# Float64 weights become float32 with three VectorE operations per piece in place of five

## The chip, the cores and the metric

The kernel runs on one core of a Trainium2 chip. The metric is the device time of one launch in microseconds (us), of which the median of three runs is taken. In the views of the profile PE is TensorE, PEld its weight loads, DVE is VectorE, ACT is ScalarE, POOL is GpSimd, and SP is the queue engine that issues most DMAs here; a name with q at its end (SPq) is the engine's sequencer.

## The reference

Attention over 12,288 tokens of 128 channels with pooled keys and values (768 keys), and behind it two expert layers, each with 2,048 hidden units. The four weight matrices of the experts arrive as float64.

```python
kv_pool = kv.reshape(B, H // r, r, W // r, r, C).mean(axis=(2, 4))
k = v = kv_pool.reshape(B, -1, C) @ w_sr
a = softmax(q @ k.transpose(0, 2, 1) / sqrt(C))
x = a @ v
h = x @ moe_w_in
x = (h * clip(h + 3, 0, 6) / 6) @ moe_w_out
h = x @ moe2_w_in
g = where(h >= 1, h, where(h <= -1, 0, (h + 1) ** 2 / 4))
out = g @ moe2_w_out
```

## The kernel before

**Products.** Each operand of a product is split into a rounded part (hi) and the rest (lo), and three products (hi·hi, hi·lo, lo·hi) accumulate in PSUM. So each pair of hidden blocks costs 6 matmuls of 128x128 by 128x512 into the layer and 6 out of it.

**Slots.** Tokens go in 24 blocks of 512, hidden units in 8 pairs of 128 per block. The main loop (`slot`, L582) runs over slots T: slot T does pair T of the first layer, pair T-11 of the second (so the second layer starts at slot 11), and a piece of attention for a later block. The order in which each engine gets its instructions is written out by hand and kept: in a slot ACT applies relu (L498), DVE multiplies (`mul1`, L504), ACT rounds the result (L532), POOL subtracts to get the lo part (L533); for the attention piece DVE takes the row maximum (L375), ACT the exponential (L400) and a scaled copy (L414), DVE the rest of that copy (L421). The second layer has `clip2` (L511), `sq2` (L517) and `max2` (L521). Each L504 needs the relu of its slot, the relu needs the matmuls L457, and these need a free PSUM buffer (there are four, given back by L504 and L521).

**Weights.** A piece of weights is 128 x 512 float64, loaded as pairs of 32-bit words into a staging buffer. There are 16 such jobs, j0 to j15, and each runs through four stages. Stage 0 to 2 turn the bits of float64 into float32 in the staging buffer; stage 3 rounds to hi on ACT (L192) and subtracts to lo on POOL (L194). Jobs j0 to j6 are placed among the steps before slot 0 (`PROLOGUE`, where `j4.2` means stage 2 of job 4); jobs j7 to j15 start in slots 0, 1, 4, 6, 7, 8, 10, 12 and 14 (`CONV_AT`). `conv_step` (L201), near the end of each slot, moves every running job by one stage, the oldest first, and then starts the new one. So a job that starts in slot T has its stages 1, 2 and 3 in slots T+1, T+2 and T+3. Behind `conv_step` a slot has only loads and matmuls, so the next thing on DVE is the softmax scale (two tiny operations, L408 and L411) and L504 of slot T+1, and on ACT it is the relu of slot T+1.

**Stages before.** DVE: stage 0 shifts the lower word (L161, tile wr) and shifts and flips the upper one (L162, wa); stage 1 makes a mask (L172, mk); stage 2 masks (L179) and joins the sign (L181). ACT: stage 0 squares the upper word (L164, mk), stage 1 rounds wr (L169). POOL: stage 1 adds wa and wr (L174). The tiles wa, wr and mk have two buffers each. The staging tiles are called t, h, l, g or wst after the buffer that they borrow; j12 to j15 use wst, which has two buffers, so that the loads of j14 and j15 wait for stage 3 of j12 and j13.

Of the kernel before, what the change touches and what calls it, by code (L numbers as in the profile page):

```python
# [8 lines left out]
FP32 = mybir.dt.float32  # L9
F32R = mybir.dt.float32r  # L10
FP16 = mybir.dt.float16
U32 = mybir.dt.uint32
I32 = mybir.dt.int32
ACTF = mybir.ActivationFunctionType
ALU = mybir.AluOpType
AX = mybir.AxisListType

W_MIN = 3.4332275390625e-05
O2, LAG2 = 11, 2
# LOADS: order of the loads (k: keys and values, w: next weights, q: queries of a block).  # L20
# PROLOGUE: order of the steps before slot 0; the table of steps stands above the slots' loop.
# CONV_AT: slots that start a weight conversion. EARLY: slots of attention for blocks 1 and 2
# (four scores, two products with V each) and of the transpose of block 2's queries.
LOADS = "w k0 k1 w k4 k6 k2 k5 k3 w q0 k8 k7 k9 k10 k11 w w w w w q1 w w w w w w q2 w w"
KV_MODE = "DDVVPPPPPPPP"
PROLOGUE = """
# [19 lines left out]
def tile_attn_moe_moe2(  # L46
# [11 lines left out]
    """Products run as float32r: an operand is split exactly into a rounded part (hi) and the  # L58
    rest (lo), and hi*hi + hi*lo + lo*hi accumulate in PSUM. The attention weights and V are
    split the same way into float16 parts, scaled by powers of two into float16's range."""  # L60
    nc = tc.nc
# [52 lines left out]
    # Jobs that end before slot 0 may use any staging buffer, those that end before slot O2 the  # L114
    # ones of the second layer, and the rest their own.
# [4 lines left out]
    # A staging buffer may be taken again once the last reader of what it holds is issued.  # L120
# [33 lines left out]
    # The upper words, read as float32, keep the order of the magnitudes: those whose square  # L154
    # reaches W_MIN ** 2 belong to weights of 2 ** -126 and more; others become zero.
    def w_stage0(job):
        t = wst[job][0]
        a = wk_p.tile([128, WP], U32, tag="wa", name="wa")
        r = wk_p.tile([128, WP], U32, tag="wr", name="wr")
        mk = wk_p.tile([128, WP], FP32, tag="mk", name="mk")  # L160
        nc.vector.tensor_scalar(out=r, in0=t[:, :, 0], scalar1=28, scalar2=None, op0=ALU.logical_shift_right)  # L161
        nc.vector.tensor_scalar(out=a, in0=t[:, :, 1], scalar1=3, scalar2=0x40000000,  # L162
                                op0=ALU.logical_shift_left, op1=ALU.bitwise_xor)
        nc.scalar.activation(out=mk, in_=t[:, :, 1].bitcast(FP32), func=ACTF.Square)  # L164
        wcv[job] = (a, r, mk)

    def w_stage1(job):
        a, r, mk = wcv[job]
        nc.scalar.activation(  # L169
            out=r.bitcast(I32), in_=r.bitcast(I32), func=ACTF.Copy, scale=0.5, bias=0.25  # L170
        )
        nc.vector.tensor_scalar(out=mk.bitcast(I32), in0=mk, scalar1=W_MIN ** 2, scalar2=-1.0,  # L172
                                op0=ALU.is_ge, op1=ALU.mult)
        nc.gpsimd.tensor_tensor(out=a.bitcast(I32), in0=a.bitcast(I32), in1=r.bitcast(I32), op=ALU.add)  # L174

    def w_stage2(job):
        a, r, mk = wcv.pop(job)
        hi32 = wst[job][0][:, :, 1]
        nc.vector.scalar_tensor_tensor(out=a, in0=a, scalar=0x7FFFFFFF, in1=mk.bitcast(U32),  # L179
                                       op0=ALU.bitwise_and, op1=ALU.bitwise_and)  # L180
        nc.vector.scalar_tensor_tensor(out=hi32, in0=hi32, scalar=0x80000000, in1=a,  # L181
                                       op0=ALU.bitwise_and, op1=ALU.bitwise_or)
# [136 lines left out]
    # DRAM rows are read and written in runs of 32 channels, so that transposes of 32 x 32  # L319
    # blocks within a partition group make [tokens, channels] from [channels, tokens] and back.  # L320
# [202 lines left out]
    def hi_lo(m, s):  # L523
        g = g_t.pop((m, s))
        # After the first layer's last pair the second one takes its buffers too.
        n = 1 if m == 0 or (s >= NS - O2 and s % 2) else 2
        hi = hl_p.tile([128, 2, 512], F32R, tag=f"h{n}", name=f"h{n}")
        lo = hl_p.tile([128, 2, 512], F32R, tag=f"l{n}", name=f"l{n}")
        hl_t[m, s] = hi, lo
        for k in range(2):  # L530
            eng = nc.vector if s == NS - 1 else nc.gpsimd
            nc.scalar.copy(out=hi[:, k], in_=g[:, k])  # L532
            eng.tensor_tensor(out=lo[:, k], in0=g[:, k], in1=f32(hi[:, k]), op=ALU.subtract)  # L533

# [1 line left out]
    # Slot T: pair T of the first layer, pair T - O2 of the second, and a piece of attention.  # L536
# [172 lines left out]
```

## Time and profile before

| | us |
|---|---|
| median of three runs | 1375.62 |
| lowest, highest | 1374.92, 1380.48 |
| the profiled execution, first to last instruction (span) | 1373.8 |

| engine | busy us | share of the span |
|---|---|---|
| PE | 1317.9 | 96% |
| DVE | 1188.8 | 87% |
| POOL | 1084.1 | 79% |
| ACT | 1033.1 | 75% |

The span of the profiled execution is 1.8 us under the median. The shares of the whole span say little about the change, since the weights are converted in the first 200 us only: there the loop has other limits than later, and the rows below cut the span at the points where these change. A row of the timeline gives the start of an instruction, its length, engine, line, operation and shape; in brackets stands the idle time of the engine ahead of it and what ended it. An instruction's length includes the time in which it was held up after it had started.

### The profile page before, as it was taken

To read this page: it belongs to the slowest core of one execution; us is meant where nothing else is said; L and a number is where in the kernel's file an instruction comes from. 1 tells how busy PE (TensorE), PEld (TensorE's weight loads), DVE (VectorE), ACT (ScalarE), POOL (GpSimd) and SP (SyncE) were. 2 spreads that over 40 slices of the span, in tenths; PEclk is the share of its full clock that TensorE was granted. 3 is DMA by queue.
4 is the path that set the end of the run, shared out by engine and by line. 5 is a ranking of instruction groups with operands and counts; after the bars stand their busy time and mean duration, and the time that the engine had idled before them with its cause. 6 is when DMAs were issued, how large, how long until landed. Compare 5 with 4: busy or idle time off the path is not lost.

```text
span 1373.8 us, 18492 instructions
## 1 busy us (share of the span) xinstructions
PE 1317.9 (96%) x6244; PEld 1077.0 (78%) x6244; DVE 1188.8 (87%) x1847; ACT 1033.1 (75%) x1917; POOL 1084.1 (79%) x826
## 2 busy tenths in 40 slices
PE   7478889999999999999999999999999999999998
PEld 6356668888888888888888888888888888888876
DVE  4899998789989989889888888898899899898777
ACT  2566787887777777777877777777877778777776
POOL 2367898888878878878878878888788788788887
PEclk9789899999999999999999999999999999999999
DMA  9442212212212122122222213222122121211000
GB/s 323 103 96 45 62 31 43 46 34 44 43 32 50 31 42 49 34 43 39 43 43 39 43 31 51 32 42 50 27 47 42 32 50 24 43 37 30 8 8 16
DMA packets 260783, 66.28 MB, mean 48 GB/s; under 512 B 252368, under 2 KB 256592, under 8 KB 260688
## 3 DMA queue, kind: packets, MB, share of 16 engines
q1 hardware_dynamic: 259456, 62.94, 23.2%
q10 hardware_dynamic: 1232, 2.16, 0.4%
q8 instruction: 49, 0.80, 0.2%
q14 instruction: 46, 0.38, 0.1%
HBM read 21.04 MB, written 6.29 MB: 20 GB/s over the span
## 4 chain that ended last, share of the span: by engine, by line
PE 86%; DVE 9%; issue 2%; ACT 1%; POOL 1%; DMA 1%; SPq 0%; DVEq 0%; POOLq 0%; ACTq 0%
PE acc L473 36%; PE h L457 36%; PE s L364 6%; PE s L436 6%; DVE wa L179 1%; PE h L245 1%; DVE t L504 1%; DVE g L521 1%; DVE g L511 1%; DVE a L421 1%; DMA h<-in_moe_w_out_dram 1%; POOL l L533 1%; DVE wa L162 1%; DVE wr L161 1%; DVE nm L375 0%
## 5 line engine op out<-in xcount | busy, mean ns | idle before, releaser
L533 POOL TENSOR_TENSOR l<-g,h 128x512 fp32r<-128x512 f32 x382 | 508.3, 1351 | 213.3 <-ACT h L532 155.7
L533 POOL TENSOR_TENSOR l<-t,h 128x512 fp32r<-128x512 f32 x382 | 501.8, 1335 | 24.6 <-ACT h L532 20.7
L498 ACT ACTIVATE t<-h 128x512 f32<-128x512 f32 x384 | 226.7, 597 | 215.5 <-PE h L457 207.6
L504 DVE SCALAR_TENSOR_TENSOR t<-t,h 128x512 f32<-128x512 f32 x384 | 248.6, 681 | 121.1 <-ACT t L498 121.0
L521 DVE TENSOR_TENSOR g<-h,g 128x512 f32<-128x512 f32 x384 | 245.6, 680 | 13.2 <-ACT g L517 6.4
L532 ACT CAST h<-t 128x512 fp32r<-128x512 f32 x384 | 224.9, 619 | 31.0 <-DVE t L504 27.7
L511 DVE TENSOR_SCALAR g<-h 128x512 f32<-128x512 f32 x384 | 245.8, 680 | 0.7 <-POOL l L533 0.4
L517 ACT ACTIVATE g<-g 128x512 f32<-128x512 f32 x384 | 228.1, 628 | 1.6 <-DVE g L511 1.3
L532 ACT CAST h<-g 128x512 fp32r<-128x512 f32 x384 | 217.7, 617 | 4.2 <-DVE g L521 3.6
L457 PE MATMUL h<-xh,wi0h 128*128 128x512 f32 x384 | 153.8, 400 | 9.2 <-DVE t L504 4.7
L473 PE MATMUL acc<-h,wo0h 128*128 128x512 f32 x384 | 156.5, 408 | 2.2 <-DVE su L408 2.2
L473 PE MATMUL acc<-l,wo0h 128*128 128x512 f32 x384 | 153.6, 400 | 4.8 <-POOL l L533 4.7
L457 PE MATMUL h<-xl,wi0h 128*128 128x512 f32 x384 | 153.7, 400 | 3.3 <-DVE xl L442 3.3
L457 PE MATMUL h<-x2h,wi1h 128*128 128x512 f32 x384 | 152.8, 398 | 2.2 <-DVE g L521 2.2
L457 PE MATMUL h<-xh,wi0l 128*128 128x512 f32 x384 | 152.9, 398 | 0.0
L473 PE MATMUL acc<-h,wo0l 128*128 128x512 f32 x384 | 152.5, 397 | 0.0
L457 PE MATMUL h<-x2h,wi1l 128*128 128x512 f32 x384 | 152.5, 397 | 0.0
L473 PE MATMUL acc<-h,wo1h 128*128 128x512 f32 x384 | 151.9, 396 | 0.6 <-DVE o L489 0.4
L457 PE MATMUL h<-x2l,wi1h 128*128 128x512 f32 x384 | 152.1, 396 | 0.0
L473 PE MATMUL acc<-l,wo1h 128*128 128x512 f32 x384 | 151.4, 395 | 0.0
L473 PE MATMUL acc<-h,wo1l 128*128 128x512 f32 x384 | 151.4, 394 | 0.0
L421 DVE SCALAR_TENSOR_TENSOR a<-e,rc,a 128x768 f16<-128x768 f32 x96 | 137.7, 1434 | 2.8
(139 smaller groups left out, 2171.7 us busy)
## 6 DMA issues: line engine op xcount, KB each, us to landing
q<-in_q_dram SPq DMA_DIRECT2D x96, 64.0 KB, 2.5
out_dram<-o SPq DMA_DIRECT2D x96, 64.0 KB, 1.9
h<-in_kv_dram SPq DMA_DIRECT2D x4, 512.0 KB, 8.9
l<-in_moe_w_in_dram SPq DMA_DIRECT2D x3, 512.0 KB, 8.7
at<-a SPq DMA_TRANSPOSE x96, 3.6
g<-in_moe_w_in_dram SPq DMA_DIRECT2D x2, 512.0 KB, 6.6
h<-in_moe_w_out_dram SPq DMA_DIRECT2D x2, 512.0 KB, 9.3
l<-in_kv_dram ACTq DMA_DIRECT2D x2, 512.0 KB, 10.4
```

The costliest lines, as they stand in the source:

```text
L364: nc.tensor.matmul(ps[h], l[:, js], r[:, ks], start=(n == 0), stop=(n == 2))
L421: nc.vector.scalar_tensor_tensor(out=a[:, 1], in0=e, scalar=rc, in1=a[:, 0], op0=ALU.mult, op1=ALU.subtract)
L436: nc.tensor.matmul(ps, l[:, k, :], r[:, k, :], start=(n == 0), stop=(n == 3 * KC - 1))
L457: nc.tensor.matmul(ps, l[:, ws], r, start=(n == 0), stop=(n == 2))
L473: nc.tensor.matmul(acc[m], l[:, ws], r[:, k, :], start=(c == 0 and i == 0), stop=(c == NPAIR - 1 and i == 5))
L498: nc.scalar.activation(out=g_t[0, s][:, k], in_=h_t[0, s, k], func=ACTF.Relu, scale=1.0 / 6.0, bias=0.5)
L504: nc.vector.scalar_tensor_tensor(out=g, in0=g, scalar=1.0, in1=h_t.pop((0, s, k)), op0=ALU.min, op1=ALU.mult)
L511: nc.vector.tensor_scalar(out=g_t[1, s][:, k], in0=h_t[1, s, k], scalar1=1.0, scalar2=-1.0, op0=ALU.min, op1=ALU.max)
L517: nc.scalar.activation(out=g, in_=g, func=ACTF.Square, scale=0.5, bias=0.5)
L521: nc.vector.tensor_tensor(out=g, in0=h_t.pop((1, s, k)), in1=g, op=ALU.max)
L532: nc.scalar.copy(out=hi[:, k], in_=g[:, k])
L533: eng.tensor_tensor(out=lo[:, k], in0=g[:, k], in1=f32(hi[:, k]), op=ALU.subtract)
```

## The change

Stage 0 now has no work for DVE: ACT takes the magnitude of the upper word (Abs, into wa) and reads one byte of each lower word, of which it makes a rounded small integer (Copy with scale and bias, into wr). Stage 1 has a clamp from below (max) and a pair of shifts on DVE, and the same addition on POOL. Stage 2 has only the operation that joins the sign. The tile mk is gone. Comments and the docstring are dropped; everything else stays.

```diff
     def w_stage0(job):
         t = wst[job][0]
         a = wk_p.tile([128, WP], U32, tag="wa", name="wa")
-        r = wk_p.tile([128, WP], U32, tag="wr", name="wr")
-        mk = wk_p.tile([128, WP], FP32, tag="mk", name="mk")
-        nc.vector.tensor_scalar(out=r, in0=t[:, :, 0], scalar1=28, scalar2=None, op0=ALU.logical_shift_right)
-        nc.vector.tensor_scalar(out=a, in0=t[:, :, 1], scalar1=3, scalar2=0x40000000,
-                                op0=ALU.logical_shift_left, op1=ALU.bitwise_xor)
-        nc.scalar.activation(out=mk, in_=t[:, :, 1].bitcast(FP32), func=ACTF.Square)
-        wcv[job] = (a, r, mk)
+        r = wk_p.tile([128, WP], I32, tag="wr", name="wr")
+        nc.scalar.activation(out=a.bitcast(FP32), in_=t[:, :, 1].bitcast(FP32), func=ACTF.Abs)
+        low = t.rearrange("p a b -> p (a b)").bitcast(U8).rearrange("p (a b) -> p a b", b=8)
+        nc.scalar.activation(
+            out=r, in_=low[:, :, 3], func=ACTF.Copy, scale=1.0 / 32.0, bias=1.0 / 64.0
+        )
+        wcv[job] = (a, r)
 
     def w_stage1(job):
-        a, r, mk = wcv[job]
-        nc.scalar.activation(
-            out=r.bitcast(I32), in_=r.bitcast(I32), func=ACTF.Copy, scale=0.5, bias=0.25
-        )
-        nc.vector.tensor_scalar(out=mk.bitcast(I32), in0=mk, scalar1=W_MIN ** 2, scalar2=-1.0,
-                                op0=ALU.is_ge, op1=ALU.mult)
-        nc.gpsimd.tensor_tensor(out=a.bitcast(I32), in0=a.bitcast(I32), in1=r.bitcast(I32), op=ALU.add)
+        a, r = wcv[job]
+        nc.vector.tensor_scalar(out=a.bitcast(FP32), in0=a.bitcast(FP32), scalar1=W_MIN,
+                                scalar2=None, op0=ALU.max)
+        nc.vector.tensor_scalar(out=a, in0=a, scalar1=5, scalar2=2,
+                                op0=ALU.logical_shift_left, op1=ALU.logical_shift_right)
+        nc.gpsimd.tensor_tensor(out=a.bitcast(I32), in0=a.bitcast(I32), in1=r, op=ALU.add)
 
     def w_stage2(job):
-        a, r, mk = wcv.pop(job)
+        a, r = wcv.pop(job)
         hi32 = wst[job][0][:, :, 1]
-        nc.vector.scalar_tensor_tensor(out=a, in0=a, scalar=0x7FFFFFFF, in1=mk.bitcast(U32),
-                                       op0=ALU.bitwise_and, op1=ALU.bitwise_and)
-        nc.vector.scalar_tensor_tensor(out=hi32, in0=hi32, scalar=0x80000000, in1=a,
+        nc.vector.scalar_tensor_tensor(out=hi32, in0=hi32, scalar=0xC0000000, in1=a,
                                        op0=ALU.bitwise_and, op1=ALU.bitwise_or)
```

On DVE, the end of slot 5, slot 6 and the start of slot 7 stand in a row like this before (l2_410 is the staging buffer of job 9, l2_497 that of job 10; t1 is the tile of the first layer's hidden values):

```order
L172 TENSOR_SCALAR mk_832<-mk_832 128x512
L504 SCALAR_TENSOR_TENSOR t1_905<-t1_905,h_901 128x512
L504 SCALAR_TENSOR_TENSOR t1_905<-t1_905,h_907 128x512
L375 TENSOR_REDUCE nm_921<-s_920 128x1
L179 SCALAR_TENSOR_TENSOR wa_830<-wa_830,mk_832 128x512
L181 SCALAR_TENSOR_TENSOR l2_410<-l2_410,wa_830 128x512
L161 TENSOR_SCALAR wr_935<-l2_497 128x512
L162 TENSOR_SCALAR wa_934<-l2_497 128x512
L408 TENSOR_SCALAR su_922<-su_922 128x1
L411 RECIPROCAL rc_957<-su_922 128x1
```

and now (the buffers of jobs 9 and 10 are l2_397 and l2_481, and line numbers behind L165 are those of the changed file; L172 is the max, L174 the shifts):

```order
L172 TENSOR_SCALAR wa_803<-wa_803 128x512
L174 TENSOR_SCALAR wa_803<-wa_803 128x512
L504 SCALAR_TENSOR_TENSOR t1_876<-t1_876,h_872 128x512
L504 SCALAR_TENSOR_TENSOR t1_876<-t1_876,h_878 128x512
L375 TENSOR_REDUCE nm_892<-s_891 128x1
L181 SCALAR_TENSOR_TENSOR l2_397<-l2_397,wa_803 128x512
L408 TENSOR_SCALAR su_893<-su_893 128x1
L411 RECIPROCAL rc_925<-su_893 128x1
```

Four conversion operations between two L504 have become one, and the one of the slot before has become two.

On ACT, the end of slot 4 and slot 5 before (stage 3 of job 8, then the start of job 9):

```order
L192 CAST wi1h_102<-h2_350 128x512
L164 ACTIVATE mk_832<-l2_410 128x512
L498 ACTIVATE t1_846<-h_842 128x512
L498 ACTIVATE t1_846<-h_848 128x512
L414 ACTIVATE a_856<-e_824,rc_853 128x768
L532 CAST h1_860<-t1_846 128x512 x2
L441 ACTIVATE xh_888<-h_869,csc_112 128x256
L169 ACTIVATE wr_831<-wr_831 128x512
L498 ACTIVATE t1_905<-h_901 128x512
```

and now:

```order
L192 CAST wi1h_102<-h2_341 128x512
L163 ACTIVATE wa_803<-l2_397 128x512
L165 ACTIVATE wr_804<-l2_397 128x512
L498 ACTIVATE t1_817<-h_813 128x512
L498 ACTIVATE t1_817<-h_819 128x512
L414 ACTIVATE a_827<-e_797,rc_824 128x768
L532 CAST h1_831<-t1_817 128x512 x2
L441 ACTIVATE xh_859<-h_840,csc_112 128x256
L498 ACTIVATE t1_876<-h_872 128x512
```

The rounding copy has moved from behind the relu of slot 5 to ahead of it; both ACT operations of a job now stand in the slot that starts it.

On POOL the order stays, and what the addition waits for changes. Before (slots 5 and 6):

```order
L533 TENSOR_TENSOR l1_861<-t1_846,h1_860 128x512 [waits PE_49,Activation_49]
L533 TENSOR_TENSOR l1_861<-t1_846,h1_860 128x512 [waits Activation_49]
L174 TENSOR_TENSOR wa_830<-wa_830,wr_831 128x512 [waits Activation_49]
L533 TENSOR_TENSOR l1_915<-t1_905,h1_914 128x512 [waits PE_49,Activation_49]
L533 TENSOR_TENSOR l1_915<-t1_905,h1_914 128x512 [waits Activation_49]
```

and now:

```order
L533 TENSOR_TENSOR l1_832<-t1_817,h1_831 128x512 [waits PE_49,Activation_49]
L533 TENSOR_TENSOR l1_832<-t1_817,h1_831 128x512 [waits Activation_49]
L176 TENSOR_TENSOR wa_803<-wa_803,wr_804 128x512 [waits DVE_49]
L533 TENSOR_TENSOR l1_886<-t1_876,h1_885 128x512 [waits PE_49,Activation_49]
L533 TENSOR_TENSOR l1_886<-t1_876,h1_885 128x512 [waits Activation_49]
```

The addition waited for ACT and now waits for DVE, whose shifts end the slot there.

## Rows read from the trace of the kernel before

**Rows 1.** By stretch: length, busy (count) of PE, PEld, DVE, ACT, POOL; PEclk, DMA.

```profile
0.00:66.80 66.80, 41.54 (x262) 34.21 (x262) 43.66 (x86) 27.59 (x60) 21.66 (x21) 0.88 0.73 218
66.80:144.10 77.30, 57.93 (x242) 44.85 (x240) 74.19 (x93) 51.25 (x93) 55.23 (x36) 0.88 0.33 67
144.10:189.80 45.70, 40.60 (x179) 32.09 (x180) 45.26 (x64) 35.12 (x65) 38.67 (x27) 0.90 0.21 49
189.80:1373.80 1184.00, 1177.83 (x5566) 965.87 (x5563) 1025.65 (x1606) 919.13 (x1699) 968.55 (x743) 1.00 0.21 37
```

**Rows 2.** DVE's busy time from 66.8 to 189.8, of line 161 alone; columns: stretch, busy (count), PEclk, DMA.

```profile
66.80:189.80 123.00, 9.18 (x9) 0.89 0.28 60
```

**Rows 3.** The same of line 162 alone.

```profile
66.80:189.80 123.00, 9.22 (x9) 0.89 0.28 60
```

**Rows 4.** Groups by line, DVE, 66.8 to 189.8: busy us, mean ns, idle before.

```profile
L179 DVE SCALAR_TENSOR_TENSOR wa<-wa,mk 128x512 uint32<-128x512 uint32 x10 | 11.9, 1187 | 0.4 <-POOL wa L174 0.4
L172 DVE TENSOR_SCALAR mk<-mk 128x512 int32<-128x512 f32 x9 | 11.7, 1303 | 0.0
```

**Rows 5.** As Rows 2, of line 181 alone.

```profile
66.80:189.80 123.00, 15.68 (x10) 0.89 0.28 60
```

**Rows 6.** Timeline of DVE, slots 1 to 7; columns: start, length, instruction.

```profile
79.95 1.50 DVE L162 TENSOR_SCALAR wa<-h 128x512 uint32<-128x512 uint32 x1
81.37 0.14 DVE L408 TENSOR_SCALAR su<-su 128x1 f32<-128x1 f32 x1
...
101.42 1.50 DVE L161 TENSOR_SCALAR wr<-l 128x512 uint32<-128x512 uint32 x1
...
104.55 1.26 DVE L504 SCALAR_TENSOR_TENSOR t<-t,h 128x512 f32<-128x512 f32 x2
...
113.97 0.41 DVE L161 TENSOR_SCALAR wr<-l 128x512 uint32<-128x512 uint32 x1
...
114.90 0.67 DVE L504 SCALAR_TENSOR_TENSOR t<-t,h 128x512 f32<-128x512 f32 x1
```

**Rows 7.** Timeline of ACT at the ends of slots 4, 6 and 14.

```profile
101.34 0.67 ACT L164 ACTIVATE mk<-l 128x512 f32<-128x512 f32 x1
101.92 1.07 ACT L498 ACTIVATE t<-h 128x512 f32<-128x512 f32 x2
...
111.73 1.07 ACT L498 ACTIVATE t<-h 128x512 f32<-128x512 f32 x2
...
171.31 0.66 ACT L164 ACTIVATE mk<-wst 128x512 f32<-128x512 f32 x1 [1.90 <-DMA wst<-in_moe_w_out_dram]
```

**Rows 8.** Timeline of DVE at the end of slot 14.

```profile
172.26 1.48 DVE L161 TENSOR_SCALAR wr<-wst 128x512 uint32<-128x512 uint32 x1
...
175.34 1.27 DVE L504 SCALAR_TENSOR_TENSOR t<-t,h 128x512 f32<-128x512 f32 x2
```

**Rows 9.** Timeline of POOL ahead of slot 0.

```profile
55.30 1.25 POOL L174 TENSOR_TENSOR wa<-wa,wr 128x512 int32<-128x512 int32 x1 [7.57 <-issue]
...
57.78 1.71 POOL L174 TENSOR_TENSOR wa<-wa,wr 128x512 int32<-128x512 int32 x1
59.45 1.72 POOL L340 TENSOR_TENSOR ql<-qT,qh 128x512 fp32r<-128x512 f32 x1
```

**Rows 10.** Timeline of DVE ahead of slot 0.

```profile
56.58 1.78 DVE L179 SCALAR_TENSOR_TENSOR wa<-wa,mk 128x512 uint32<-128x512 uint32 x1 [3.03 <-POOL wa L174]
...
61.75 1.66 DVE L181 SCALAR_TENSOR_TENSOR g<-g,wa 128x512 uint32<-128x512 uint32 x1
...
64.01 0.86 DVE L442 SCALAR_TENSOR_TENSOR xl<-h,csc,xh 128x256 fp32r<-128x256 f32 x2
...
66.81 0.69 DVE L504 SCALAR_TENSOR_TENSOR t<-t,h 128x512 f32<-128x512 f32 x1
```

**Rows 11.** Lines 164 and 169 by form, whole run: duration ns min/median/max, first and last start.

```profile
L164 ACT ACTIVATE mk<-l x5: 655/673/685, 21.5 to 111.2; 128x512 f32<-128x512 f32 x5
...
L169 ACT ACTIVATE wr<-wr x16: 613/629/645, 7.3 to 180.0; 128x512 int32<-128x512 int32 x16
```

More of the change, by code (lines that the diff above doesn't have):

```diff
@@ L13 @@
 I32 = mybir.dt.int32
+U8 = mybir.dt.uint8
 ACTF = mybir.ActivationFunctionType
```

## The prediction, made before the changed kernel ran

> **What bounds the kernel now.** I read the busy time by stretch first, cut at slot 0 (66.8 us), slot 11 (144.1) and the last conversion (189.8) [rows 1]. Behind 189.8 PE is busy 1177.8 of 1184.0 us at full clock: no other engine can shorten that. From 66.8 to 189.8 it is different: DVE is busy 74.19 + 45.26 = 119.4 of 123.0 us, while PE has 98.5 us (at a mean clock of 0.88 to 0.90), POOL 93.9 and ACT 86.4. Here DVE sets the pace, and time taken from it reaches the end of the run one to one, as long as nothing else comes late. This is where nine of the sixteen conversions lie. Ahead of 66.8 DVE is busy 43.7 of 66.8 us, and what conversions cost there has to be found on the chain that leads to slot 0.
>
> Next I read what conversions take of DVE from 66.8 to 189.8: L161 9.18 us in 9 instructions [rows 2], L162 9.22 [rows 3], L172 11.7 and L179 11.9 (10, since job 6 ends there) [rows 4], L181 15.68 in 10 [rows 5]. Together 57.7 us, nearly half of the stretch, and mostly not arithmetic: the same operation of the same shape takes 0.41 us in one place and 1.50 us in another [rows 6]. The long ones run while POOL works, so they are waits for POOL that count as busy time. The price of an operation here is whether POOL is running when it starts.
>
> **What goes (DVE).** Per job, L161 and L162 leave stage 0 and L179 leaves stage 2. From 66.8 on that is 9.18 + 9.22 + 11.87 = 30.3 us; neighbours overlap by 0.08 us (79.95 + 1.50 = 81.45, and the next one starts at 81.37 [rows 6]), 28 times 0.08 is 2.2, so **28.0 us** go.
>
> **What comes (DVE).** The max takes the place, source type and shape of L172: no difference. The shifts behind it are new, nine of them. Bounds are the 0.41 and 1.50 of such an operation [rows 6]: 3.7 to 13.5 us. The nearest row is L162, which also follows another one-source operation directly: 9.22 / 9 = 1.02 each [rows 3], **9.2 us**. A gain from it is excluded, since it is added.
>
> **L181's price.** It stood behind L179 and cost 15.68 / 10 = 1.57; now it stands first, where L179 cost 1.19 [rows 4, 5]. Between the two (0 and 3.8 us in ten) I take half, **1.9 us** gained, because some of the places have POOL busy throughout. DVE is thus relieved by 28.0 - 9.2 + 1.9 = **20.7 us**, with ends at 28.0 - 13.5 = 14.5 and 28.0 - 3.7 + 3.8 = 28.1.
>
> **What is late next.** ACT's count per job stays (Square and Copy become Abs and Copy), but the Copy moves one slot forward, ahead of the relu on which L504 of the next slot rests. Queued behind it on ACT are that relu, the softmax copy and the roundings for POOL; DVE and then PE wait for these. In the slots that start a job next to no other ACT conversion work left, this shows. Slot 4: without L161 and L162 DVE is through at 101.42, and two tiny operations (0.14 for one) lead to L504, say 101.7; the relu begins at 101.92, half a microsecond later with one more operation (0.55, as 101.34 to 101.92), and needs 0.6: L504 at 103.1 instead of 104.55 [rows 6, 7]. So 1.4 of the relief is not passed on. Slot 6: relu 111.73 + 0.55 + 0.6 = 112.9, while DVE would be there one L181 (1.57) and the pair (2 x 0.33, starts apart) before 114.90, at 112.7 [rows 5 to 7]: 0.2. Slot 14: the load of job 15 lands at 171.3 and ACT waits 1.90 us for it; Abs, Copy, relu give L504 at 173.0, where it stood at 175.34; DVE would be ready at 172.26 less an L179 (1.19) and the tiny ones later, at 171.3 [rows 4, 7, 8]: 1.7. The mean of these is 1.1; five slots (0, 4, 6, 10, 14) have this pattern: **5.5 us** lost. In the slots where the Copy leaves, ACT gains as much, which brings nothing as DVE is later there.
>
> POOL's addition waited for ACT and now waits for the shifts. Queued behind it are the two or four subtractions of the next slot, which wait for L504 of that slot anyway, and L504 comes after the shifts. So I cost it at nothing; without that cover it costs POOL one shift, 0.41 to 1.5 us, nine times (below, third rival).
>
> **Ahead of slot 0.** POOL is out of use until 55.30 (7.57 us that nothing in the view explains) and does its addition of job 4 then [rows 9]; that I leave. From there DVE runs without a gap through L179, L181, L179, L181, L161, L162 to the lo part of the first input at 64.01, on which the first product and so L504 at 66.81 rest [rows 10]. Two L179, L161 and L162 go. L181 of job 5 needs the addition that ends at 59.49 and then waits for L340, which begins at 59.45 and takes 1.28 of its 1.72 us itself: it ends at 61.4, and the lo part starts there instead of at 64.01 [rows 9, 10]. That is **2.7 us**, between 1.0 (the max and the shifts of job 6, now ahead of slot 0, wait for POOL) and 3.5 (L181 gets in ahead of L340 and takes 1.0). What goes earlier hides behind loads, the pooling on PE and POOL's pause.
>
> **The sum.** 20.7 - 5.5 + 2.7 = 17.9 us of the profiled execution's 1373.8: a span of 1355.9. The median lies 1.8 us over the span, so **1357.7**. PE allows it: its gaps from 66.8 to 189.8 are 24.5 us [rows 1], without counting that it ran part of the matmuls below full clock. With 0.5% (6.9 us) as what a measurement of this kernel can tell, that is faster.
>
> **First rival: POOL holds every operation up.** If each remaining operation meets a running POOL instruction, the relief is the low end, 14.5 - 5.5 + 2.7 = 11.7: 1363.9. For it: POOL would be busy 94 us of about 107. Against: POOL can't have its addition running while it waits for the shifts, so in several slots the shifts find it idle. The Trainium skill has this as a rule (SBUF — State Buffer, § Who interferes with whom): VectorE and GpSimd share one pair of SBUF ports, an operation of VectorE that uses both ports or has two SBUF inputs and a GpSimd operation exclude each other for the whole instruction, and the later one blocks. The trace agrees, by the 0.41 and 1.50 us of the same shift. Chance 0.20.
>
> **Second rival: the whole relief arrives.** Shifts at 0.41, L181 at 1.19, half of ACT's loss: 28.1 - 2.7 + 2.7 = 28.1, 1347.5. Against: it needs more than PE's 24.5 us of gaps, so PE's slow pieces would have to go too. Chance 0.12.
>
> **Third rival: the new wait eats it.** If POOL is the next bound and its subtractions come late by a shift at its long price each time, 9 x 1.5 = 13.5 of the 17.9 are lost: 1371.2, within 0.5%. Against: POOL has 29 us of idle time from 66.8 to 189.8. Chance 0.06.
>
> **Fourth rival, on the other side: bytes on ACT.** No row shows ACT reading one byte in eight. Its nearest rows are L169 (dense, 629 ns) and L164 (every second word, 660 to 673) [rows 11]: a stride costs 0.03 to 0.04, and I take L169's 0.63. If the Copy takes x us more, the five slots where ACT is late lose x each and the four others (1, 7, 8, 12) x minus about 1.0 of slack, an estimate from slot 4's margins. It decides from 5x + 4(x - 1) = 17.9, x = 2.4, a Copy of 3.0 us. At seven times L169 (4.4 us, x = 3.8) 30 us are lost: 1388. The Trainium skill speaks against it (ScalarE: Activation LUTs, § ACT is a hardware spline evaluator): one element per cycle and lane whatever the function, measured in fp32 and bf16; no run here shows it for bytes; by it the sum stands. Chance 0.04.
>
> **How the numbers follow.** The sum 0.58, the rivals 0.20, 0.12, 0.06, 0.04. Left out are the third and fourth rival (0.10), half of the second (0.06) and the far side of the first (0.04): 1349 to 1366. Faster by over 0.5% (under 1368.7): 0.58 + 0.20 + 0.12 = 0.90; within: 0.06; slower: 0.04. That the change doesn't do what it says is not a case: the rows of the three engines show five DVE operations per job become three.
>
> **What would show it.** In the changed kernel's profile slot 0's L504 should start near 64.1; DVE's busy time between there and the last L181 should fall by some 20 us; the shifts should show two prices, 0.4 and 1.5; L181 a mean below 1.57; ACT's two stage-0 operations 0.6 to 0.7 us each; L504 of slots 5 and 15 should wait for the relu. The PE-bound stretch should begin about 18 us earlier and keep its length. I am wrong if ACT's Copy is long, if POOL shows idle time that ends with the shifts and PE waits for L533 behind it, or if DVE stays as busy per slot as now.

## The result and the profile after

The changed kernel takes **1354.33 us** (median of four runs, 1353.61 to 1357.25) against 1375.27 of the kernel before beside it: a ratio of 0.9845, 95% interval [0.9818, 0.9873]. Measured again later it took 1356.07 (five runs, 1353.82 to 1363.06), a ratio of 0.9867 [0.9839, 0.9896]. The prediction was 1357.7 with a range of 1349 to 1366, and a chance of 0.90 that it would be faster by over 0.5%; both intervals lie beyond that.

The profiled execution of the changed kernel has a span of 1355.5 us (before: 1373.8). By stretch, cut at slot 0, slot 11 and slot 17, the counterpart of [rows 1] (columns as there):

```profile
0.00:63.50 63.50, 40.69 (x263) 33.74 (x264) 33.85 (x73) 27.65 (x60) 19.07 (x21) 0.89 0.80 229
63.50:129.20 65.70, 55.71 (x240) 42.99 (x239) 57.27 (x79) 51.13 (x94) 52.91 (x37) 0.90 0.38 78
129.20:170.20 41.00, 37.38 (x164) 29.58 (x165) 39.88 (x59) 35.51 (x65) 37.78 (x27) 0.96 0.25 55
170.20:1355.50 1185.30, 1179.39 (x5580) 967.15 (x5578) 1025.60 (x1606) 919.47 (x1699) 969.46 (x744) 1.00 0.21 37
```

Between slot 0 and slot 17 DVE, the third pair of numbers, is busy 57.27 + 39.88 = 97.15 us, where it was 74.19 + 45.26 = 119.45 [rows 1]. PE behind slot 17 is as full as before. TensorE's mean granted clock in slots 0 to 17 rose from 0.89 [rows 2] to 0.92; that is not where the gain comes from, since DVE was idle for only 3.6 of the 123 us before, and a faster PE could have taken no more than that from it. The time went from the first 190 us. The span splits into four parts. The loads of keys and values end about where the last pooling copy (L266) starts on ACT; from there to slot 0's L504 the prologue finishes; then come slots 0 to 17, and the rest, where PE is the bound:

| us | before | after | difference |
|---|---|---|---|
| start to the beginning of the last L266 | 35.35 | 34.53 | -0.8 |
| to L504 of slot 0 | 31.46 | 29.04 | -2.4 |
| slots 0 to 17 | 123.02 | 106.70 | -16.3 |
| slot 17 to the end | 1183.97 | 1185.20 | +1.2 |
| span | 1373.8 | 1355.5 | -18.3 |

The first part is not the change's: in all profiled runs of this study it lies between 32.3 and 35.4 us, in two executions of the same changed kernel at 34.53 and 32.34. It is why spans alone can't settle 2 us here, and why I compare the middle two parts, which agree in those two executions within 0.5 us (29.04 and 28.89; 106.70 and 106.27).

The nine shifts of the changed kernel in slots 0 to 17 (L174), its nine max (L172), its ten joins (L181), busy time alone, in this order; the counterparts are [rows 2 to 5]:

```profile
63.50:170.20 106.70, 9.72 (x9) 0.92 0.33 70
...
63.50:170.20 106.70, 10.45 (x9) 0.92 0.33 70
...
63.50:170.20 106.70, 12.31 (x10) 0.92 0.33 70
```

Two pieces of DVE's timeline, slot 8 and slot 9, show the two prices of the shifts:

```profile
113.91 1.51 DVE L172 TENSOR_SCALAR wa<-wa 128x512 f32<-128x512 f32 x1
115.45 0.43 DVE L174 TENSOR_SCALAR wa<-wa 128x512 uint32<-128x512 uint32 x1
...
120.47 1.51 DVE L172 TENSOR_SCALAR wa<-wa 128x512 f32<-128x512 f32 x1
122.02 1.42 DVE L174 TENSOR_SCALAR wa<-wa 128x512 uint32<-128x512 uint32 x1
```

and POOL's timeline beside them:

```profile
112.15 2.98 POOL L533 TENSOR_TENSOR l<-t,h 128x512 fp32r<-128x512 f32 x2
115.96 1.28 POOL L176 TENSOR_TENSOR wa<-wa,wr 128x512 int32<-128x512 int32 x1 [0.82 <-DVE wa L174]
118.34 3.36 POOL L533 TENSOR_TENSOR l<-t,h 128x512 fp32r<-128x512 f32 x2 [1.10 <-ACT h L532]
121.66 1.49 POOL L194 TENSOR_TENSOR wi1l<-l,wi1h 128x512 fp32r<-128x512 f32 x1
```

At 115.45 POOL is through with L533 (112.15 + 2.98 = 115.13) and its addition L176 waits for this very shift, which takes 0.43. At 122.02 POOL is inside L194 until 123.15: the shift takes 1.42. In slots 0 to 17 three shifts take 0.43 and six 1.39 to 1.43.

What DVE waits for between slot 0 and slot 17, before and then after (columns: what waits, on what, total us, times, longest):

```profile
DVE t L504 <- ACT t L498: 0.6, 1, 0.6
...
DVE t L504 <- ACT t L498: 7.0, 6, 2.3
```

So DVE has 22.3 us less to do, its idle time grows from 3.6 to 9.6 us, and 16.3 arrive. The largest of the new waits, at slot 11 (DVE), with what ACT does ahead of it at the end of slot 10:

```profile
129.22 1.29 DVE L504 SCALAR_TENSOR_TENSOR t<-t,h 128x512 f32<-128x512 f32 x2 [2.26 <-ACT t L498]
...
127.48 0.66 ACT L163 ACTIVATE wa<-wst 128x512 f32<-128x512 f32 x1
128.05 0.65 ACT L165 ACTIVATE wr<-wst 128x512 int32<-128x512 uint8 x1
128.60 1.06 ACT L498 ACTIVATE t<-h 128x512 f32<-128x512 f32 x2
```

The relu of slot 11 stands behind both operations of the new job; L163 is the magnitude and L165 the byte copy. The byte copy's durations over the whole run (ns, min/median/max), the counterpart of [rows 11]:

```profile
L165 ACT ACTIVATE wr<-l x5: 646/666/679, 21.3 to 103.4; 128x512 int32<-128x512 uint8 x5
L165 ACT ACTIVATE wr<-g x4: 645/652/660, 7.5 to 108.3; 128x512 int32<-128x512 uint8 x4
```

### The profile page after: what moved, and what is told of

It reads as the page before. It is cut to its first block, busy times and chain, and to the rows that moved or that the text cites. A ratio compares the mean times of both kernels' runs of the same rounds, so it can differ in the third digit from the quotient of the medians.

```text
span 1355.5 us, 18465 instructions
## 1 busy us (share of the span) xinstructions
PE 1313.2 (97%) x6244; PEld 1073.5 (79%) x6244; DVE 1156.6 (85%) x1815; ACT 1033.8 (76%) x1917; POOL 1079.2 (80%) x826
## 4 chain that ended last, share of the span: by engine, by line
PE 87%; DVE 4%; POOL 1%; ACT 1%; issue 1%; DMA 0%; ACTq 0%; DVEq 0%; POOLq 0%
PE acc L473 37%; PE h L457 37%; PE s L364 7%; PE s L436 6%; POOL l L533 1%; DVE t L504 1%; DVE a L421 1%; DVE nm L375 1%; DVE wa L172 0%; ACT t L498 0%; DVE g L181 0%; DVE wa L174 0%; DMA wst<-in_moe_w_out_dram 0%; ACT a L414 0%; DVE g L511 0%
## 5 line engine op out<-in xcount | busy, mean ns | idle before, releaser
L533 POOL TENSOR_TENSOR l<-g,h 128x512 fp32r<-128x512 f32 x382 | 507.9, 1351 | 210.0 <-ACT h L532 150.6
L533 POOL TENSOR_TENSOR l<-t,h 128x512 fp32r<-128x512 f32 x382 | 501.2, 1334 | 10.5 <-ACT h L532 7.1
L504 DVE SCALAR_TENSOR_TENSOR t<-t,h 128x512 f32<-128x512 f32 x384 | 248.7, 682 | 128.2 <-ACT t L498 128.2
L532 ACT CAST h<-t 128x512 fp32r<-128x512 f32 x384 | 225.1, 620 | 35.2 <-DVE t L504 31.9
L517 ACT ACTIVATE g<-g 128x512 f32<-128x512 f32 x384 | 228.0, 628 | 1.7 <-DVE g L511 1.7
L532 ACT CAST h<-g 128x512 fp32r<-128x512 f32 x384 | 217.7, 617 | 4.2 <-DVE g L521 3.6
L421 DVE SCALAR_TENSOR_TENSOR a<-e,rc,a 128x768 f16<-128x768 f32 x96 | 137.2, 1429 | 3.3 <-ACT a L414 0.5
```

Source lines behind the costliest of these rows:

```text
L421: nc.vector.scalar_tensor_tensor(out=a[:, 1], in0=e, scalar=rc, in1=a[:, 0], op0=ALU.mult, op1=ALU.subtract)
L504: nc.vector.scalar_tensor_tensor(out=g, in0=g, scalar=1.0, in1=h_t.pop((0, s, k)), op0=ALU.min, op1=ALU.mult)
L517: nc.scalar.activation(out=g, in_=g, func=ACTF.Square, scale=0.5, bias=0.5)
```

## The experiments

All are edits of the changed kernel. My theory: DVE sets the pace in slots 0 to 17, what it is relieved of arrives there but for ACT's lateness, and the price of a DVE operation is whether POOL is running. The rivals: the changed order of ACT or POOL's new wait decides, or the prices have another cause. The ratios are against the kernel before on the same chip; the three stretches are of the profiled runs, in us.

| run | median | ratio, 95% interval | L266 to slot 0 | slots 0 to 17 | slot 17 to end |
|---|---|---|---|---|---|
| before | 1375.27 | 1 | 31.46 | 123.02 | 1184.0 |
| after | 1354.33 | 0.9845 [0.9818, 0.9873] | 29.04 | 106.70 | 1185.2 |
| after, again (e12) | 1356.07 | 0.9867 [0.9839, 0.9896] | 28.89 | 106.27 | 1185.5 |
| e1: pair back | 1370.91 | 0.9969 [0.9958, 0.9981] | 32.00 | 119.26 | 1184.1 |
| e2: mask back | 1365.48 | 0.9936 [0.9923, 0.9948] | 30.54 | 116.02 | 1184.3 |
| e3: no shifts | 1348.29 | 0.9817 [0.9791, 0.9842] | 28.39 | 99.73 | 1185.3 |
| e4: byte copy later | 1352.64 | 0.9843 [0.9825, 0.9860] | 28.50 | 104.63 | 1185.2 |
| e5: byte copy twice | 1360.62 | 0.9898 [0.9885, 0.9911] | 29.09 | 111.82 | 1184.1 |
| e6: addition free | 1356.92 | 0.9864 [0.9850, 0.9879] | 28.40 | 107.79 | 1185.1 |
| e7: stages 1, 2 between | 1375.63 | 1.0012 [0.9995, 1.0029] | 29.15 | 126.33 | 1191.2 |
| e8: e7 and copy later | 1371.80 | 0.9973 [0.9962, 0.9985] | 29.05 | 121.55 | 1186.2 |
| e9: stage 1 between | 1358.45 | 0.9882 [0.9851, 0.9913] | 28.55 | 107.37 | 1186.7 |
| e10: e9 and copy later | 1356.63 | 0.9865 [0.9841, 0.9888] | 28.19 | 105.92 | 1186.4 |
| e11: POOL narrow | 1345.62 | 0.9785 [0.9750, 0.9820] | 28.86 | 95.61 | 1184.9 |

### The terms, one by one: e1, e2, e3

e1 puts two one-source DVE operations back into stage 0, into a buffer that nobody reads:

```diff
     def w_stage0(job):
+        jk = wk_p.tile([128, WP], U32, tag="jk", name="jk")
+        nc.vector.tensor_scalar(out=jk, in0=t[:, :, 0], scalar1=28, scalar2=None, op0=ALU.logical_shift_right)
+        nc.vector.tensor_scalar(out=jk, in0=t[:, :, 1], scalar1=3, scalar2=0x40000000,
+                                op0=ALU.logical_shift_left, op1=ALU.bitwise_xor)
```

> The changed kernel with two one-source VectorE operations put back into stage 0, of the form of the old L161 and L162; they write a scratch tile that nobody reads. My theory (VectorE sets the pace from slot 0 to slot 17, and the removed pair was worth its waits for GpSimd): the pair's 18.4 us less overlap in the slots, minus the 5 us or so that ScalarE hides in the slots that start a job, plus 0.7 ahead of slot 0: 10 to 14 us slower than the changed kernel, 1364 to 1368. The rival that the gain comes from elsewhere (stage 2, or less waiting on GpSimd's side): under 4 us slower, at most 1358.

It lost 16.6 us, more than the 10 to 14 of the theory. Slots 0 to 17 took 12.6 longer: DVE's busy time there, the third pair of numbers, rose by 18.6, and its waits for the relu almost vanished (L508 is the multiplication, L502 the relu in this kernel):

```profile
66.20:185.40 119.20, 96.78 (x411) 74.46 (x410) 115.72 (x154) 87.25 (x159) 92.32 (x64) 0.90 0.28 62
...
DVE t L508 <- ACT t L502: 1.4, 3, 0.6
```

That is 18.6 more work and 5.6 less waiting, 13.0 for the 12.6 measured. The waits of the changed kernel are thus what DVE's relief laid bare, not something that the moved copy adds by itself. The prologue lost 3.0, where the expectation had 0.7.

e2 puts a two-source operation back ahead of L181:

```diff
     def w_stage2(job):
+        jk = wk_p.tile([128, WP], U32, tag="jk", name="jk")
+        nc.vector.scalar_tensor_tensor(out=jk, in0=a, scalar=0x7FFFFFFF, in1=hi32,
+                                       op0=ALU.bitwise_and, op1=ALU.bitwise_and)
```

> The changed kernel with one VectorE operation with two SBUF sources put back ahead of the last operation of stage 2, of the form of the old L179; it writes a scratch tile that nobody reads. My theory: in the slots ten times 1.0 to 1.5 us, of which some hides behind ScalarE, and 3 us ahead of slot 0, where two of them lie between the addition and the first product: 9 to 14 us slower than the changed kernel, 1363 to 1368. The rival that only the number of one-source operations counts: under 4 us slower.

It lost 11.2 us, as expected in all: 9.3 in the slots, and 1.5 in the prologue, where 3 were expected. L181 (L184 in this kernel), now second again, costs what it cost before (15.68 [rows 5]):

```profile
65.80:181.80 116.00, 15.63 (x10) 0.91 0.30 64
```

against 12.31 after: behind another two-source operation it pays 0.33 more than first in the row.

e3 leaves the shifts out:

```diff
     def w_stage1(job):
-        nc.vector.tensor_scalar(out=a, in0=a, scalar1=5, scalar2=2,
-                                op0=ALU.logical_shift_left, op1=ALU.logical_shift_right)
```

> The changed kernel without the pair of shifts of stage 1, so that the weights come out with wrong values; everything else runs. The shifts take 9.1 us start to start in the slots of the changed kernel, in five places 1.3 to 1.4 us and in four 0.35. My theory: 5 to 8 us faster than the changed kernel (1346 to 1349), since some of it meets ScalarE or GpSimd next. If GpSimd's instructions are the true bound and a VectorE operation only waits where time is free, under 2 us.

As expected: 6.0 us faster. (The nine shifts of these slots are six long and three short, not five and four.) Of the shifts' 9.72 us in the slots 7.0 arrive; the wait for the relu grows from 7.0 to 9.3 us. One after the other the parts don't add up: 12.6 + 9.3 - 7.0 - 2.1 (e4, next) = 12.8 of the 16.3. These runs don't resolve the 3.5 left. That the prices shift with each edit is a likely part of it, not shown to be all: the max takes 10.5 us after, 11.7 in e1 and 8.3 in e2.

### ACT: e4, e5

e4 takes the byte copy back to stage 1, where the kernel before rounded; e5 makes it twice in stage 0, the second into a buffer that nobody reads:

```diff
     def w_stage0(job):
-        nc.scalar.activation(
-            out=r, in_=low[:, :, 3], func=ACTF.Copy, scale=1.0 / 32.0, bias=1.0 / 64.0
-        )
     def w_stage1(job):
+        nc.scalar.activation(
+            out=r, in_=low[:, :, 3], func=ACTF.Copy, scale=1.0 / 32.0, bias=1.0 / 64.0
+        )
```

> The changed kernel with the Copy of the bytes moved from stage 0 back to stage 1, behind the relu of the next slot, where the old rounding stood. My theory of what is late next (relu one ScalarE operation later in slots 0, 4, 6, 10 and 14): 0.55 us in each of them come back, 2 to 3 us faster than the changed kernel, 1351 to 1352. The rival that the loss in these slots is not ScalarE's order (a transfer, TensorE): within 1 us of the changed kernel.

```diff
     def w_stage0(job):
+        jk = wk_p.tile([128, WP], I32, tag="jk", name="jk")
+        nc.scalar.activation(
+            out=jk, in_=low[:, :, 3], func=ACTF.Copy, scale=1.0 / 32.0, bias=1.0 / 64.0
+        )
```

> After the change plus a second copy of the same byte view on ScalarE, into a scratch buffer, right behind the first. It prices ScalarE's slack in stage 0. The changed kernel takes 1354.3 us. Theory (ScalarE is late next): L504 waits there for the relu of the slot in slots 1, 5, 7, 8, 11 and 15, and a further operation of some 0.65 us adds about its length to those waits and opens a few in other slots: 2 to 4 us slower, 1356.5 to 1358.5, with the start of L504 in slot 17 at 172 to 174 us in place of 170.3. Rival (ScalarE has slack nearly everywhere): under 1 us slower, below 1355.5.

e4's slots take 104.63, 1.6 to 2.1 less than in the two executions of the changed kernel, and its multiplication (L505) waits 4.9 us for the relu in place of 7.0:

```profile
DVE t L505 <- ACT t L499: 4.9, 7, 1.7
...
DVE t L508 <- ACT t L502: 10.2, 7, 2.8
```

The second line is e5's. In the median e4 takes 1352.64, but the intervals of the ratios overlap: a gain of 2 us is seen in the trace and not established in the time. e5 lost 6.3 us, more than my 2 to 4: the slots took 5.1 longer, of which the rows name 3.2 in longer waits for the relu (10.2 against 7.0 us) and 1.1 in a dearer max (11.6 against 10.5). In the five slots that the prediction named each wait grew by 0.5 to 0.7 us. Of the four others, to which it gave a slack of about 1.0 us, an estimate, one opened: L504 of slot 13 now waits 0.54, so there the slack was too large.

### POOL: e6 and e11

e6 makes POOL's addition independent of the shifts: it reads and writes wr alone, and L181 joins wr, so that the weights come out wrong.

```diff
     def w_stage1(job):
-        nc.gpsimd.tensor_tensor(out=a.bitcast(I32), in0=a.bitcast(I32), in1=r, op=ALU.add)
+        nc.gpsimd.tensor_tensor(out=r, in0=r, in1=r, op=ALU.add)
     def w_stage2(job):
-        nc.vector.scalar_tensor_tensor(out=hi32, in0=hi32, scalar=0xC0000000, in1=a,
+        nc.vector.scalar_tensor_tensor(out=hi32, in0=hi32, scalar=0xC0000000, in1=r.bitcast(U32),
```

> After the change, with POOL's addition made independent of the shifts: it adds to the random buffer in place, and the last VectorE operation joins the buffer that the addition leaves. The rounding bits are not the reference's in this kernel: the weights are left without the shifted byte, and all instructions keep their number and shape. The changed kernel takes 1354.3 us. Theory (the new wait of the addition on the shift is idle time of POOL that ends nothing): within 1 us, 1353.3 to 1355.3. Rival (the wait delays L181 and through it the weights): 3 to 10 us faster, 1344 to 1351. Third (an earlier addition meets the shift itself on the shared port and lengthens it): 1 to 3 us slower.

The time is that of the changed kernel (0.9864 against 0.9845 and 0.9867), so POOL's new wait costs nothing. The rows show why, and something else. Line 174 between slots 0 and 17 in e6 (ns, min/median/max):

```profile
L174 DVE TENSOR_SCALAR wa<-wa x9: 1144/1399/1425, 73.0 to 163.2; 128x512 uint32<-128x512 uint32 x9
```

All nine shifts are long now, 11.88 us together in place of 9.72. The three that were short meet the addition itself, which starts 0.36 us ahead of them, and take 1.14 to 1.15, as in slot 2:

```profile
81.59 1.15 DVE L174 TENSOR_SCALAR wa<-wa 128x512 uint32<-128x512 uint32 x1
...
81.23 1.22 POOL L176 TENSOR_TENSOR wr<-wr 128x512 int32<-128x512 int32 x1
```

Its slots take 1.1 to 1.5 us longer than in the two executions of the changed kernel, as the third possibility of the expectation had it; in the time this is not established. In the changed kernel the wait for the shift keeps POOL's addition away from it.

e11 measures the price itself. L533, POOL's subtraction behind each layer, (L532 here) is cut to one column, and the products read the rounded part in its place:

```diff
     def hi_lo(m, s):
-        hl_t[m, s] = hi, lo
+        hl_t[m, s] = hi, hi
         for k in range(2):
-            eng.tensor_tensor(out=lo[:, k], in0=g[:, k], in1=f32(hi[:, k]), op=ALU.subtract)
+            nc.gpsimd.tensor_tensor(out=lo[:, k, :1], in0=g[:, k, :1], in1=f32(hi[:, k, :1]), op=ALU.subtract)
```

> After the change, with POOL's subtraction behind each layer (L533) cut to one column of 512, and the products that read its result reading the high part instead: the low part of the hidden values is left out. POOL is then idle beside the conversion but for its additions and the weights' low parts. It measures the disputed price alone. Theory (a one-source or two-source VectorE operation of the conversion is long where an operation of POOL runs beside it): L172 and L174 take 0.40 to 0.45 us in all slots but one or two, and VectorE's busy time between slots 0 and 17 falls by 10 to 20 us. Rival (the long ones come from ScalarE or from the data they read, whatever POOL does): means of L172 and L174 stay at 1.0 to 1.2 us. The time itself may fall or rise by some us, since the matrix products no longer wait for POOL, and is not what the run is for.

DVE's busy time in the slots, the third pair of numbers, falls by 16.6, from 97.15 to 80.58, with every one of its instructions still there (138 in both):

```profile
63.60:159.20 95.60, 86.75 (x401) 69.55 (x400) 80.58 (x138) 85.91 (x158) 39.73 (x65) 0.95 0.38 78
```

The joins take 0.65 to 0.69 each. Of the 18 max and shifts 12 are short (0.41 to 0.43) and six long (1.03 to 1.55), more than the one or two expected, since POOL's other operations were left as they were: each of the six runs beside one of them, L194 or L340. In DVE's timeline of this run, slots 2 and 9:

```profile
78.01 0.42 DVE L172 TENSOR_SCALAR wa<-wa 128x512 f32<-128x512 f32 x1
78.46 1.40 DVE L174 TENSOR_SCALAR wa<-wa 128x512 uint32<-128x512 uint32 x1
...
112.67 1.55 DVE L172 TENSOR_SCALAR wa<-wa 128x512 f32<-128x512 f32 x1
114.25 0.43 DVE L174 TENSOR_SCALAR wa<-wa 128x512 uint32<-128x512 uint32 x1
```

and in POOL's:

```profile
78.25 1.33 POOL L340 TENSOR_TENSOR ql<-qT,qh 128x512 fp32r<-128x512 f32 x1 [1.31 <-ACT qh L339]
...
112.25 1.68 POOL L194 TENSOR_TENSOR wi1l<-l,wi1h 128x512 fp32r<-128x512 f32 x1 [0.72 <-ACT wi1h L192]
```

The long shift ends at 79.86, 0.28 after POOL's operation (79.58); the long max at 114.22, 0.29 after it (113.93). That the long ones are waits for POOL is shown by this, and by the 16.6 us. It is the rule that the prediction cited (the Trainium skill, SBUF — State Buffer, § Who interferes with whom): the later of the two blocks for the other's whole instruction.

### Using it: e7 to e10

If the place sets the price, the conversion's operations should stand where POOL is idle, between the two L504 of a slot. e7 moves DVE's part of stages 1 and 2 there, e9 that of stage 1 alone:

```diff
     def slot(T):
-            for k in range(2):
-                mul1(s1, k)
+            mul1(s1, 0)
+            conv_dve()
+            mul1(s1, 1)
```

Here `conv_dve` issues L172 and the shifts of the jobs in stage 1 (and in e7 the join of those in stage 2); POOL's addition stays behind. e8 and e10 are these two with the byte copy in stage 1, as in e4.

> After the change, with VectorE's part of stages 1 and 2 of a slot moved to between the two L504 operations of the slot, in place of behind both. It computes the same. The changed kernel takes 1354.3 us. Theory (a VectorE operation is long where POOL is in an operation of its own, so that the place in the slot sets its price): shifts at 1.4 us and L172, L181 at 1.1 to 1.5 us become short in more slots, 4 to 9 us faster, 1345 to 1350, with slots 0 to 17 at 98 to 103 us in place of 106.7. Rival (the weights come later for L504's second operation, or ScalarE's relu ends the wait instead): within 2 us, or slower.

> The run before (VectorE's part of stages 1 and 2 between the two L504 operations) and the byte copy back in stage 1, where the kernel before had it. It computes the same. Alone the copy in stage 1 took 1352.6 us against 1354.3. Theory (the two act on different terms: the place of the VectorE operations, and ScalarE ahead of the first relu): 1 to 3 us faster than the run before it, 1343 to 1348, with the start of L504 in slot 0 near 60.8 us. Rival (they act on the same wait): equal to the better of the two alone.

The shifts and the max became cheap, 3.8 and 5.9 us in e7 for 9.7 and 10.5, and yet the whole gain of the change was lost, where 4 to 9 us more were expected. What DVE waits for in e7, slots 0 to 17 (L188 is the join, L179 the addition, L523 the multiplication, L517 the relu):

```profile
DVE t L523 <- ACT t L517: 15.3, 12, 2.3
DVE wst L188 <- POOL wa L179: 8.8, 4, 3.1
DVE x2l L500 <- ACT x2h L499: 3.0, 2, 2.7
DVE su L427 <- ACT e L419: 2.6, 3, 1.1
DVE h L188 <- POOL wa L179: 2.3, 2, 1.4
DVE l L188 <- POOL wa L179: 1.8, 2, 1.2
```

The addition stands behind POOL's subtractions of the slot before, and a join this early waits for it, 13.2 us in all (the three buffers shown and 0.3 on the fourth), ahead of an L504 that everything waits for. The profiled execution of e7 is 7.9 us over its median, and most of that lies behind slot 17 (1191.2 us for 1184 to 1187 in the others); the 126.33 us of the slots are enough to see the loss.

> After the change, with VectorE's part of stage 1 alone (L172 and the shifts) between the two L504 of a slot; L181 stays behind both, POOL's addition where it stood. It computes the same. With stage 2 moved too the kernel took 1375.6 us, since L181 then waited 14.3 us for POOL's addition, while L172 and the shifts fell from 20.7 to 10.2 us between 63 and 200 us. Theory (the wait of L181 ate the gain, the place of the shifts was right): 1346 to 1351 us, slot 17 starts at 161 to 166 us in place of 170.3, and L181 waits for POOL under 3 us in all. Rival (the second L504 of a slot, 0.9 us later, delays POOL's subtraction and the next slot): within 1.5 us of 1354.3, or slower. Third (L181 takes up what the shifts give, now meeting POOL's later addition): L181's mean goes to 1.6 us or over and the time stays within 2 us.

> The run before, and the byte copy of ScalarE back in stage 1, where the kernel before had it. It computes the same. Alone the copy in stage 1 gave 1.7 us. Theory (two different terms): 1 to 3 us faster than the run before it, with slot 0 near 60.8 us. Rival (POOL's addition now waits for the copy, which stands behind ScalarE's work of the slot, and L181 waits for the addition): slower than the run before it by 1 to 8 us, with L181 waiting for POOL's addition in most slots.

With the join left behind, that wait is gone (none in e9's slots), the max and the shifts fall from 20.2 to 12.1 us, and still nothing arrives: 107.37. The relief of 8.1 was given back to others. The scaled copy behind the two L504, L421, is one of them; its ten instructions in slots 0 to 17, in the changed kernel, in e9, and in e11, where POOL is busy 39.73 of the 95.6 us:

```profile
63.50:170.20 106.70, 14.91 (x10) 0.92 0.33 70
...
61.00:168.30 107.30, 17.90 (x10) 0.95 0.32 69
...
63.60:159.20 95.60, 10.11 (x10) 0.95 0.38 78
```

It takes 3.0 more than in the changed kernel. The waits for the relu (L513 in e9) grow by 4.0, from 7.0 to 11.0, and a wait of 1.8 for ACT's copy x2h is new:

```profile
DVE t L519 <- ACT t L513: 11.0, 9, 2.2
DVE x2l L496 <- ACT x2h L495: 1.8, 1, 1.8
```

Together 8.8 us came back for the 8.1 saved, and the slots took 0.7 longer. e10 gains 1.4 on e9 in the slots, e8 4.8 on e7; in both pairs only the copy's place differs. Of the versions that compute the same, none is established as faster than the changed kernel.

> The changed kernel itself, beside the two versions with moved steps, so that differences of 1 to 3 us are read on one chip: 1353 to 1357 us. If it takes 1354.3 again, the 2.6 us more of the run with the free addition are its own; if it takes 1356 or more, they are not.

The second measurement of the changed kernel, 1356.07, removes the 2.6 us by which e6 seemed slower, and leaves e10 level with it and e9 2.4 us behind, inside its spread (1353.82 to 1363.06).

## The prediction, step by step

**What bounds the kernel: right.** 22.3 us less work for DVE in slots 0 to 17 made these 16.3 us shorter, and e1 and e2 gave most of it back. Behind slot 17 nothing shortened, as forecast; that stretch even grew by 1.2 us (see the sum).

**What goes and what comes: right in kind, a little short.** The pair was 18.4 us [rows 2, 3], and put back in e1 a pair adds 18.6 to DVE's busy time. The shifts were priced at 9.2 and took 9.72, with the two prices foretold. The max was to cost what L172 cost [rows 4] and took 10.45 for 11.7. L181 was to gain 1.9 and gained 15.68 - 12.31 = 3.4, nearly the upper end of 3.8: first behind the slot's work it costs 1.23, close to L179's 1.19. The scaled copy L421, which the prediction left as it was, took 14.91 for 14.29:

```profile
66.80:189.80 123.00, 14.29 (x10) 0.89 0.28 60
```

Together DVE's relief was 28.0 - 9.7 + 1.2 + 3.4 - 0.6 = 22.3, not 20.7.

**What is late next: right, with the loss 0.5 larger.** The five slots named (0, 4, 6, 10, 14) are those behind which L504 waits: 0.74, 1.31, 1.28, 2.26 and 0.90 us at slots 1, 5, 7, 11 and 15, 6.5 together. The 0.53 that makes it 7.0 is at slot 8, where the relu itself waited for PE (0.62). DVE's whole idle time grew by 6.0, where I had 5.5 lost. The size per slot was less good (that an ACT operation delays the relu by 0.55 is 0.58 by its own row, which moves nothing): slot 6 was given 0.2 and cost 1.28; slot 14 was given 1.7, much of it the 1.90 us that ACT waited there for a load, and cost 0.90, with 0.62 of that wait left. The errors nearly cancel, which is luck. That POOL's new wait costs nothing was shown by e6.

**Ahead of slot 0: right in the path, near in the number by luck.** 2.7 forecast (its own times give 64.01 - 61.4 = 2.6), 2.4 and 2.6 measured from the end of the loads. The forecast counts from POOL's addition of job 4, and from there to slot 0 it is 3.1: 66.81 - 55.30 = 11.51 us before, 63.57 - 55.17 = 8.40 after, and 8.40 again in e12.

```profile
55.17 1.25 POOL L176 TENSOR_TENSOR wa<-wa,wr 128x512 int32<-128x512 int32 x1 [7.09 <-issue]
```

Of the 3.1, 2.8 lie ahead of the lo part, and 0.3 between it and L504, where DVE works without a gap. But this addition came 0.5 to 0.7 later behind the loads than before, for a reason that these runs don't show. In the changed kernel the join of job 5 starts at 59.40 as soon as its addition is done, and the lo part of the input at 61.07 (61.4 forecast, 64.01 before [rows 10]), in DVE's timeline:

```profile
59.40 1.75 DVE L181 SCALAR_TENSOR_TENSOR g<-g,wa 128x512 uint32<-128x512 uint32 x1 [1.17 <-POOL wa L176]
61.07 0.86 DVE L442 SCALAR_TENSOR_TENSOR xl<-h,csc,xh 128x256 fp32r<-128x256 f32 x2
...
63.57 0.68 DVE L504 SCALAR_TENSOR_TENSOR t<-t,h 128x512 f32<-128x512 f32 x1
```

**The sum.** 20.7 - 5.5 + 2.7 = 17.9 was forecast. Measured: 16.3 in the slots where 15.2 was forecast, 2.4 ahead of them, 0.8 of earlier loads that the change doesn't own, less 1.2 given back behind slot 17, which I had at nothing: 18.3. That it stands so near 17.9 is in part luck. The 1.2 is a step that failed, a small one: the stretch behind the cut did not keep its length. The rows give the reason. The cut is an instruction of DVE, and the run ends with PE's work; behind the cut PE has 5580 matmuls in the changed kernel and 5566 in the one before [rows 1], 1179.39 us of work and 1177.83. So DVE's way to slot 17 was 16.3 us shorter, but PE had 14 matmuls more still to do there, and they fill the 1.2 us. The others agree: before, e1, e2 and e5 have 1184.0 to 1184.3 us and 5566 to 5575 matmuls behind slot 17; after, e3, e4, e6 and e11 have 1184.9 to 1185.5 us and 5580 to 5583. e8 to e10 have 1186.2 to 1186.7 us and 5583 to 5587; e7 has 1191.2 us with 5580, and so something else besides, which stays open.

**The rivals.** The first (POOL holds every operation up) is refuted for the reason given: the addition can't run while it waits for the shifts, so some are short; e6 takes that protection away and all nine are long. The second (all of the relief arrives) fell twice: only three shifts are short, so that DVE was relieved by 22.3 and not 28.1, and ACT's lateness held back 6.0 of that. The third (the new wait eats it) fell in e6. It is real elsewhere: e7 shows what the addition costs where the join stands too near behind it. The fourth fell with the byte copy's 645 to 679 ns against 613 to 645 for the dense copy [rows 11]; its point of decision was set too high, since e5 lost 5.1 us in the slots to one more copy of 0.65, where the rival's formula has 5 x 0.65 = 3.3.

## What to carry to other kernels

Read the price of an instruction where it stands: the same shift took 0.43 or 1.42 us here, by whether POOL was inside an instruction. An operation taken from the engine that sets the pace is worth its busy time less the waits on the next engine that it lays bare, and from the trace before one can tell in which slots these waits will lie; their sizes came out only in the sum. Moving an operation to where it is cheap moves the meeting to its neighbour: cheaper shifts (8.1 us) brought nothing, because the next large operation became dearer instead (L421, 3.0 us), and ACT was the next to be waited for.

## What the runs showed of the hardware

- ACT read one byte in eight of an SBUF row as 128x512 uint8 in 645 to 679 ns, against 652 to 682 ns for the float32 of every second word (L163): the byte type had no price.
- A wait of POOL made DVE faster: the shift that POOL's addition waits for took 0.43 us in three of nine slots, and 1.14 or more in all nine once the addition was free.
- DVE's busy time in slots 0 to 17 was 16.6 us shorter with POOL's subtraction cut to one column; L421 alone (128x768 into float16) took 1.01 us in place of 1.49.
- The start of the kernel varied by 3 us (32.3 to 35.4 to the end of the loads) over the profiled executions, and by 2.2 (34.53 and 32.34) between two of the same kernel.
